# Spectral mixing by full float32 products in place of three products of rounded parts

## The chip, the cores and the metric

One core of one Trainium2 chip runs the whole program. The metric is the device time of one execution in microseconds, from launch to end. TensorE (PE in the profile; PEld are its weight loads), VectorE (DVE), ScalarE (ACT), GpSimd (POOL) and SyncE (SP, which issues most transfers) each work through their own instructions in order.

## The reference

The input is `q`, `k`, `v` of shape (8, 8, 576, 64), float32, and two weight matrices. For each batch:

```
q_d, k_d, v_d = means of q, k, v over groups of 4 positions
out_d   = softmax attention of the pooled q_d, k_d, v_d      (144 positions)
local   = softmax attention within |i - j| < 4               (576 positions)
x       = repeat(out_d, 4) + local, heads side by side       -> (8, 576, 512)
mixed   = Re(FFT over 512 channels of the FFT over 576 positions of x)
u       = x + mixed
un      = layer norm of u
out     = u + relu(un @ w_ch1) @ w_ch2                        (512 -> 2048 -> 512)
```

## The kernel before

**Stages.** The first part goes batch by batch: 40 units of local attention (5 in each batch), 8 pooled attentions, and 8 spectral mixings (`Mix`). The mixed rows go to DRAM. The second part is the feed-forward network over 36 tiles of 128 tokens in 9 blocks; blocks from the fourth on use a scheme with fewer products (`product`, L1120). In the meantime the weights are unpacked in 64 quarters (`Quarter`).

**The order.** Every step is an item; the table `TURNS` gives each item a place, all items are sorted by place, and each engine works through its own in that order. Loads of the attention inputs (L574, L578) and stores stand in SyncE's queue; the constants (`constants`, L715 to L717), the pooled sums (L450) and the accumulating loads (L1019, L1023) in GpSimd's.

**Precision.** A product of type F32R is a single pass at reduced precision. The kernel gets near float32 by splitting each operand into a rounded part ("high") and the remainder ("low") and adding three products: high x high, high x low and low x high. Attention scores, probabilities times values, and transposes are plain float32 products.

**A mixing (`Mix`), for one batch.** `half_sum` (L733, VectorE, `xs`) and `half_difference` (L736, GpSimd, `xm`) add and subtract the mirrored halves of the sequence. `channels` (L744, VectorE, `w`) and `fold` (L757, one half on VectorE and one on GpSimd, `xeo`) do the same along the channels, in four slots of 128 rows. `split_high` (L768, ScalarE) rounds a folded slot to `fh`, `split_low` (L771, GpSimd) takes the remainder `fl`. `split_z` (L779 ScalarE, L780 GpSimd) does that for the two channels that are their own mirror images. `sequence` (L793) multiplies with the cosine and sine constants `seqm` along the sequence: for each of four groups T, 4 slots x 3 products of 290 columns, accumulated in PSUM. `sequence_z` (L812) does 8 products for the single channels. `sequence_high` (L800, ScalarE) rounds the result to `yh`, `sequence_low` (L804, VectorE) takes the remainder `yl`. `mix` (L832, L839) multiplies these with the channel constants `chanm`, 2 x 3 products of 256 columns for each row tile and parity; `even_out` (L846) and `unfold` (L858) combine the two parities.

Of the kernel before, what the change touches and what calls it, by code (L numbers as in the profile page):

```python
# [27 lines left out]
        0, 9, 10, 27, 42, 84, 98, 111, 152, 166, 207, 231, 226, 272, 300, 325, 370, 392, 439, 501, 529, 570,  # L28
        612, 702, 681, 707, 748, 838, 829, 841, 940, 975,
    ),  # L30
    "Pooled.scores": (
        17, 16, 47, 82, 106, 173, 217, 239, 298, 358, 386, 449, 522, 539, 582, 670, 690, 737, 821, 845, 908,
        959, 995, 1049,
    ),
    "Pooled.maxima": (
        21, 20, 52, 87, 109, 182, 221, 246, 306, 362, 389, 459, 527, 542, 590, 674, 698, 745, 825, 851, 916,
        968, 1001, 1053,
    ),
    "Pooled.exps": (
        25, 33, 57, 89, 122, 184, 234, 256, 308, 365, 396, 468, 544, 551, 608, 678, 713, 776, 832, 862, 926,  # L40
        980, 1012, 1055,
    ),
    "Pooled.transpose_p": (
        29, 48, 62, 110, 126, 188, 249, 282, 332, 385, 427, 474, 546, 566, 638, 699, 740, 782, 855, 884, 928,
        989, 1018, 1060,
    ),
    "Pooled.copy_p": (
        34, 56, 71, 120, 142, 201, 255, 285, 334, 394, 431, 478, 552, 575, 643, 709, 743, 788, 861, 898, 936,
        993, 1022, 1065,
    ),  # L50
    "Pooled.values": (
        49, 58, 90, 140, 147, 209, 281, 297, 343, 407, 434, 484, 565, 584, 657, 739, 752, 801, 883, 910, 944,
        1017, 1048, 1067,
    ),
    "Pooled.result": (
        51, 63, 94, 163, 162, 213, 290, 304, 346, 412, 446, 490, 589, 593, 661, 747, 770, 809, 888, 912, 950,
        1032, 1052, 1075,
    ),
    "Pooled.store": (151, 225, 376, 504, 650, 869, 1028, 1083),
    "Pooled.pack": (102, 228, 369, 530, 682, 830, 963, 1082),  # L60
    "Mix.half_sum": (
        132, 129, 131, 245, 220, 268, 379, 414, 413, 557, 560, 563, 696, 720, 746, 852, 850, 891, 982, 984,
        1033, 1106, 1094, 1110,
    ),
    "Mix.half_difference": (
        115, 116, 112, 237, 236, 274, 393, 416, 417, 549, 571, 580, 703, 706, 751, 842, 879, 856, 976, 977,
        1010, 1105, 1100, 1118,
    ),
    "Mix.channels": (
# [4 lines left out]
    ),  # L74
    "Mix.fold": (
# [4 lines left out]
    ),  # L80
    "Mix.split_high": (
        121, 145, 177, 176, 286, 276, 337, 336, 421, 422, 479, 477, 572, 577, 619, 622, 712, 742, 777, 791, 901,
        900, 937, 935, 991, 1014, 1046, 1066, 1122, 1137, 1168, 1169,
    ),
    "Mix.split_low": (
        139, 168, 179, 178, 301, 299, 341, 340, 438, 437, 482, 481, 579, 581, 623, 625, 732, 750, 780, 799, 904,
        902, 941, 942, 1008, 1041, 1063, 1085, 1134, 1142, 1175, 1176,
    ),
    "Mix.split_z": (119, 143, 253, 275, 395, 430, 467, 576, 640, 778, 814, 899, 992, 1056, 1064, 1117),
    "Mix.sequence_z": (175, 333, 450, 628, 784, 930, 1061, 1125),  # L90
    "Mix.z_high": (185, 338, 480, 641, 789, 934, 1116, 1136),
    "Mix.z_low": (196, 350, 491, 647, 794, 948, 1128, 1185),
    "Mix.sequence": (
        191, 187, 189, 190, 355, 359, 357, 356, 521, 523, 507, 508, 665, 671, 636, 639, 818, 820, 805, 804, 956,
        957, 970, 971, 1113, 1114, 1092, 1096, 1190, 1189, 1192, 1191,
    ),
    "Mix.sequence_high": (204, 203, 367, 363, 525, 512, 679, 646, 831, 816, 960, 981, 1123, 1124, 1215, 1212),
    "Mix.sequence_low": (211, 210, 382, 381, 540, 517, 686, 662, 835, 823, 966, 987, 1127, 1129, 1224, 1219),
# [5 lines left out]
    "Mix.even_out": (
        280, 254, 397, 423, 433, 574, 578, 711, 692, 734, 860, 859, 994, 1025, 1013, 1148, 1149, 1236, 1284,
        1308,
    ),
    "Mix.unfold": (
        305, 294, 289, 295, 410, 411, 443, 442, 463, 462, 601, 591, 599, 632, 727, 728, 767, 772, 768, 769, 889,
        887, 864, 868, 1005, 1006, 1072, 1071, 1031, 1030, 1184, 1154, 1182, 1223, 1272, 1270, 1315, 1316, 1327,  # L110
        1341,
    ),
    "Mix.store_mixed": (368, 458, 685, 826, 964, 1081, 1252, 1324),
    "Mix.store_local": (103, 157, 263, 262, 375, 455, 535, 655, 683, 762, 870, 925, 1029, 1080, 1104, 1111),
    "Mix.store_ends": (532, 962, 1078, 1357),
    "Unit.load": (
        2, 1, 4, 6, 5, 40, 39, 38, 43, 77, 101, 154, 158, 153, 159, 149, 266, 331, 264, 328, 371, 378, 454, 456,
        503, 537, 528, 618, 617, 651, 757, 760, 754, 763, 761, 874, 872, 921, 873, 922,
    ),
    "Unit.sum_in": (  # L120
        8, 11, 12, 13, 14, 53, 55, 64, 67, 78, 193, 197, 198, 199, 200, 317, 320, 347, 351, 353, 488, 489, 495,
        516, 519, 592, 602, 631, 648, 660, 796, 806, 807, 810, 811, 919, 946, 947, 951, 953,
    ),
    "Unit.load_v": (
        3, 41, 76, 75, 100, 99, 150, 155, 156, 224, 223, 227, 261, 329, 373, 372, 453, 505, 502, 531, 536, 614,
        615, 653, 652, 758, 755, 759, 828, 827, 871, 876, 875, 924, 923, 1027, 1026, 961, 1079, 1077,
    ),
# [12 lines left out]
    "Unit.transpose_p": (  # L140
        30, 31, 59, 79, 92, 93, 125, 174, 192, 216, 250, 260, 311, 310, 384, 425, 424, 485, 511, 545, 596, 597,
        637, 666, 688, 719, 718, 786, 787, 834, 844, 885, 929, 931, 969, 1020, 1019, 1088, 1058, 1095,
    ),
    "Unit.copy_p": (
        35, 36, 72, 83, 97, 118, 127, 202, 205, 230, 279, 278, 323, 324, 391, 429, 432, 498, 514, 548, 607, 606,
        644, 668, 701, 733, 735, 790, 798, 837, 858, 897, 932, 939, 973, 1023, 1024, 1089, 1062, 1097,
    ),
    "Unit.values": (
        37, 50, 81, 91, 104, 148, 172, 208, 215, 238, 313, 309, 344, 383, 399, 435, 473, 510, 538, 554, 627,
        629, 659, 687, 715, 783, 785, 819, 833, 846, 909, 915, 943, 955, 988, 1040, 1038, 1093, 1087, 1098,  # L150
    ),
    "Unit.result": (
        44, 54, 86, 96, 107, 164, 181, 212, 218, 242, 319, 315, 348, 388, 405, 447, 486, 526, 541, 561, 630,
        633, 664, 694, 726, 792, 795, 824, 836, 849, 911, 945, 949, 965, 1002, 1051, 1045, 1103, 1090, 1107,
    ),
    "constants": (28,),
    "clear_yz": (74,),
    "close_b": (1099,),
    "close_a": (1139,),
    "close_e": (1238,),  # L160
    "close_d": (1367,),
    "Block.load": (
        377, 611, 903, 534, 797, 1009, 756, 878, 974, 452, 978, 1084, 1156, 1164, 1180, 1158, 1166, 1198, 1162,
        1201, 1240, 1159, 1217, 1253, 1649, 1657, 1662, 1651, 1658, 1666, 1652, 1659, 1668, 1653, 1661, 1669,
    ),
    "Block.stats": (1070, 1073, 1091, 1119, 1206, 1221, 1269, 1271, 1667),
# [93 lines left out]
def kernel(  # L260
# [450 lines left out]
    for t in (zs.bitcast(F32), *(t[:, :, DM:] for t in halves)):  # L711
        nc.gpsimd.memset(t, 0.0)
# [749 lines left out]
```

## Time and profile before

| | |
|---|---|
| median of 3 runs | 1140.92 us (1140.8 to 1146.13) |
| the profiled execution | 1142.11 us, span 1140.3 us |
| TensorE busy | 1051.2 us, 92% |
| VectorE busy | 648.7 us, 57% |
| ScalarE, GpSimd busy | 410.1 us, 415.7 us |
| granted TensorE clock, mean | 0.976 of full |
| moved by DMA | 226.81 MB |

Busy time is the time in which an engine has at least one instruction under way. TensorE's instructions are pipelined and their ends are modelled, so its busy time is an upper figure; distances between starts say what an instruction costs in a row of others. Of the rows below, "idle before" is the time that the engine stood still ahead of the instruction, and behind "<-" stands what ended it.

### The profile page before, as it was taken

What the parts mean: (1) busy time and instruction counts of PE and PEld (TensorE: products, weight loads), DVE (VectorE), ACT (ScalarE), POOL (GpSimd) and SP (SyncE); (2) the same over time, 40 slices, a digit from 0 to 9 for tenths busy, and PEclk for the clock granted to TensorE, in tenths of its full rate; (3) what the DMA queues carried; (4) which work ended last, traced back from release to release, by engine and by line L of the source; (5) the groups of instructions that cost most, each with busy time, mean ns of one, the idle gap of its engine ahead of it and who ended that gap; (6) DMA issues with size and microseconds to landing.
All of it is one profiled execution on the core that took longest, in us unless ns stands there. A gap on an engine that the chain in (4) does not pass through costs nothing.

```text
span 1140.3 us, 24515 instructions
## 1 busy us (share of the span) xinstructions
PE 1051.2 (92%) x9364; PEld 913.5 (80%) x9364; DVE 648.7 (57%) x1314; ACT 410.1 (36%) x1138; POOL 415.7 (36%) x572
## 2 busy tenths in 40 slices
PE   5677877887889999999899999999999999999998
PEld 4566766776878888888788989989889888989997
DVE  3688998997898877354223443443343353353433
ACT  3646656765544443132121232232132132132111
POOL 2244545644575554477532131330231321222000
PEclk9888999998999999999999999999999999999999
DMA  8877878997576442668905945964974875785651
GB/s 278 236 223 207 280 197 240 284 260 183 138 188 186 129 122 93 156 208 276 236 28 182 285 152 157 269 232 159 239 249 156 231 251 183 207 265 175 218 161 37
DMA packets 124692, 226.81 MB, mean 199 GB/s; under 512 B 15104, under 2 KB 30592, under 8 KB 124320
## 3 DMA queue, kind: packets, MB, share of 16 engines
q1 hardware_dynamic: 110288, 194.51, 52.1%
q0 software_dynamic: 14288, 30.74, 14.8%
q8 instruction: 74, 1.21, 0.4%
q14 instruction: 42, 0.34, 0.1%
HBM read 179.56 MB, written 45.42 MB: 197 GB/s over the span
## 4 chain that ended last, share of the span: by engine, by line
PE 65%; DMA 12%; DVE 11%; SPq 5%; POOL 3%; issue 3%; ACT 2%; DVEq 0%; POOLq 0%; ACTq 0%
PE banks L1120 19%; PE banks L1202 10%; PE banks L1203 10%; PE banks L1204 10%; PE banks L1182 9%; DMA qkT<-in_qk_dram 2%; DMA vaug<-in_vw_dram 2%; DMA xa<-rest 1%; DVE sums L592 1%; PE banks L1049 1%; DMA w1h<-ut 1%; SPq L552 1%; DMA w1l<-ut 1%; SPq L551 1%; DMA ux<-xa 1%
## 5 line engine op out<-in xcount | busy, mean ns | idle before, releaser
L1202 PE MATMUL banks<-w2h,hh 128*128 128x512 f32 x576 | 228.6, 397 | 0.5 <-ACT hh L1186 0.5
L1203 PE MATMUL banks<-w2l,hh 128*128 128x512 f32 x576 | 226.2, 393 | 0.0
L1204 PE MATMUL banks<-w2h,hl 128*128 128x512 f32 x576 | 225.9, 392 | 0.0
L1186 ACT ACTIVATE hh<-row 128x512 fp32r<-128x512 f32 x96 | 60.8, 633 | 284.5 <-DVE row L1145 193.1
L1145 DVE TENSOR_TENSOR row<-wt,banks 128x256 f32<-128x256 f32 x192 | 80.4, 419 | 142.8 <-PE banks L1120 138.2
L1190 DVE SCALAR_TENSOR_TENSOR hl<-row,hh 128x512 fp32r<-128x512 f32 x96 | 68.8, 717 | 119.0 <-ACT hh L1186 119.0
L1204 PEld LDWEIGHTS banks<-w2h,hl 128*128 128x128 f32 x576 | 108.6, 189 | 24.8 <-DVE hl L1190 0.8
L1202 PEld LDWEIGHTS banks<-w2h,hh 128*128 128x128 f32 x576 | 108.8, 189 | 20.7 <-ACT hh L1186 0.9
L1203 PEld LDWEIGHTS banks<-w2l,hh 128*128 128x128 f32 x576 | 108.8, 189 | 19.4
L1182 PE MATMUL banks<-unT,w1h 128*128 128x512 f32 x384 | 102.1, 391 | 0.5 <-DVE unT L1058 0.5
L1019 POOL DMA_DIRECT2D ut<-ux x40 | 35.8, 1037 | 149.6 <-DMA ut<-um 144.8
L1182 PEld LDWEIGHTS banks<-unT,w1h 128*128 128x128 f32 x384 | 71.9, 188 | 16.3 <-DVE unT L1058 1.0
L1190 DVE SCALAR_TENSOR_TENSOR hl<-banks,hh 128x512 fp32r<-128x512 f32 x48 | 32.9, 687 | 79.5 <-ACT hh L1186 79.4
L628 ACT ACTIVATE sb<-banks,mx 128x64 f32<-128x64 f32 x320 | 70.2, 331 | 1.9 <-PE banks L641 0.6
L1140 ACT COPY wt<-banks 128x256 f32<-128x256 f32 x96 | 35.8, 373 | 94.2 <-PE banks L1120 94.2
L1034 POOL TENSOR_TENSOR rstd<-rstd,mhalf 128x1 f32<-128x1 f32 x36 | 21.4, 594 | 118.7 <-DVE rstd L1033 118.5
L1120 PE MATMUL banks<-w1h,w1l 128*128 128x256 f32 x384 | 62.4, 284 | 1.7 <-DMA w1l<-ut 1.2
L1120 PE MATMUL banks<-w1h,w1h 128*128 128x256 f32 x384 | 61.9, 283 | 1.8 <-DVE wt L1145 1.0
L1120 PE MATMUL banks<-unT,w1h 128*128 128x256 f32 x432 | 63.2, 282 | 0.0
L1120 PE MATMUL banks<-unT,w1l 128*128 128x256 f32 x432 | 63.2, 282 | 0.0
L1120 PEld LDWEIGHTS banks<-unT,w1h 128*128 128x128 f32 x432 | 59.9, 191 | 3.9
L1120 PEld LDWEIGHTS banks<-unT,w1l 128*128 128x128 f32 x432 | 59.8, 191 | 3.7
(127 smaller groups left out, 2102.0 us busy)
## 6 DMA issues: line engine op xcount, KB each, us to landing
w1l<-ut SPq DMA_DIRECT2D x96, 256.0 KB
w1h<-ut SPq DMA_DIRECT2D x96, 256.0 KB
qkT<-in_qk_dram SPq DMA_DIRECT2D x40, 512.0 KB
w1h<-ub SPq DMA_DIRECT2D x72, 256.0 KB
w1l<-ub SPq DMA_DIRECT2D x72, 256.0 KB
raw<-in_wq_dram SPq DMA_DIRECT2D x64, 256.0 KB
vaug<-in_vw_dram SPq DMA_DIRECT2D x40, 260.0 KB
out_dram<-ut SPq DMA_DIRECT2D x36, 256.0 KB
```

The costliest lines, as they stand in the source:

```text
L628: nc.scalar.activation(out=self.sb[:, hp, z], in_=self.sc[:, z, hp], func=AF.Exp, scale=0.125, bias=self.mx[:, z, hp : hp + 1],)
L1019: nc.gpsimd.dma_start(out=to, in_=ux[b][k0 : k0 + m, :], accum_op=ALU.add)
L1034: nc.gpsimd.tensor_tensor(out=rstd, in0=rstd, in1=mhalf, op=ALU.pow)
L1120: nc.tensor.matmul(into, w[:, y, c, :], both[z][:, c, :], start=(start and i == 0), stop=(i == len(mms) - 1), skip_group_check=True)
L1140: nc.scalar.copy(out=joins[k].bitcast(F32), in_=self.ps[x])
L1145: nc.vector.tensor_add(out=place(to), in0=place(a), in1=self.ps[x])
L1182: nc.tensor.matmul(hps, a[:, c, :], unT[:, x, c, :], start=(i == 0), stop=(i == len(mms) - 1))
L1186: nc.scalar.activation(out=hh, in_=self.hps[f], func=AF.Relu)
L1190: nc.vector.scalar_tensor_tensor(out=hl, in0=self.hps[f], scalar=0.0, in1=self.hh[f].bitcast(F32), op0=ALU.max, op1=ALU.subtract)
L1202: nc.tensor.matmul(acc, hh, w2h, start=start, stop=False)
L1203: nc.tensor.matmul(acc, hh, w2l, start=False, stop=False)
L1204: nc.tensor.matmul(acc, hl, w2h, start=False, stop=stop)
```

## The change

The mixing uses plain float32 products: one product for each pair of operands, in place of three F32R products of rounded parts. `split_high` and `split_low` go; `fold` writes the whole of `f`, which holds all four slots and has two buffers. `split_z` loses its subtraction. `sequence_high` becomes `sequence_out`, one copy of the PSUM result to `yh`, and gives the banks back; `sequence_low` goes. The constants `seqm` and `chanm` hold one part in place of two. `TURNS` has the same order of items as before, without those that are gone; `sequence_out` has the places of `sequence_high` and the numbers are closed up.

```diff
-    seqm = psq.tile([P, 2, 2, NSL + 1, KEPT], F32R, name="seqm")
-    chanm = pf.tile([P, 2, 4, HN], F32R, name="chanm")
+    seqm = psq.tile([P, 2, NSL + 1, KEPT], F32, name="seq")
+    chanm = pf.tile([P, 4, HN], F32, name="chan")
...
-    zs = psq.tile([P, NSL + 1, ZCOLS], F32R, name="z")
+    zs = psq.tile([P, NSL + 1, ZCOLS], F32, name="z")
...
         def fold(self, t, minus):
-            if self.x.get(t) is None:
-                self.x[t] = psq.tile([P, 4, P], F32, name="xeo", bufs=2)
+            if self.f is None:
+                self.f = psq.tile([P, NSL + 1, 4, P], F32, name="f", bufs=2)
...
-                out=self.x[t][:, 2 * minus : 2 * minus + 2, :],
+                out=self.f[:, t, 2 * minus : 2 * minus + 2, :],
...
-        def split_high(self, t):
-            if self.fh is None:
-                self.fh, self.fl = (psq.tile([P, NSL + 1, 4, P], F32R, name=f"f{part}", bufs=1) for part in "hl")
-            nc.scalar.copy(out=self.fh[:, t], in_=self.x[t])
-
-        def split_low(self, t):
-            nc.gpsimd.tensor_sub(out=self.fl[:, t], in0=self.x[t], in1=self.fh[:, t].bitcast(F32))
...
             nc.scalar.copy(out=z[:, :, 0:2], in_=x)
-            nc.gpsimd.tensor_sub(out=z[:, :, 2:4], in0=x, in1=z[:, :, 0:2].bitcast(F32))
-
-        def slots(self, x, odd, i):
-
-            return [(x[:, t], seqm[:, i, odd, t, :]) for t in (NSL, NSL - 1, *range(NSL - 1))]
+
+        def slots(self, x, odd):
+
+            return [(x[:, t], seqm[:, odd, t, :]) for t in (NSL, NSL - 1, *range(NSL - 1))]
 
         def sequence(self, T):
-            fh, fl = self.fh[:, :, T, :], self.fl[:, :, T, :]
...
-            mms = [x for f, i in ((fh, 0), (fh, 1), (fl, 0)) for x in self.slots(f, T % 2, i)]
+            mms = self.slots(self.f[:, :, T, :], T % 2)
...
-        def sequence_high(self, i):
+        def sequence_out(self, i):
             if self.yh is None and self.b % 2 == 0:
-                self.yh, self.yl = (pf.tile([P, 4, 2 * KEPT], F32R, name=f"y{part}", bufs=1) for part in "hl")
+                self.yh = pf.tile([P, 4, 2 * KEPT], F32, name="yf", bufs=1)
             elif self.yh is None:
-                self.yh, self.yl = mixes[self.b - 1].yh, mixes[self.b - 1].yl
+                self.yh = mixes[self.b - 1].yh
             nc.scalar.copy(out=self.yh[:, 2 * i : 2 * i + 2, self.mine], in_=self.y[i])
-
-        def sequence_low(self, i):
-            yh, yl = (y[:, 2 * i : 2 * i + 2, self.mine] for y in (self.yh, self.yl))
-            nc.vector.tensor_sub(out=yl, in0=self.y[i], in1=yh.bitcast(F32))
             done((self, i), "y")
 
         def sequence_z(self):
 
             y = self.yzp = bank(self, "yz", ZCOLS)[:, 0, :KEPT]
-            mms = [x for i in range(2) for x in self.slots(zs, 0, i)]
+            mms = self.slots(zs, 0)
...
             for half, T in enumerate((3, 1) if odd else (0, 2)):
-                mh, ml = chanm[:, 0, T, :], chanm[:, 1, T, :]
-                lh, ll = self.yh[:, T, cols], self.yl[:, T, cols]
                 to = ps[:, half * HD : (half + 1) * HD]
-                for i, (l, r) in enumerate(((lh, mh), (lh, ml), (ll, mh))):
-                    nc.tensor.matmul(
-                        to, l, r, start=(bool(odd) and i == 0), stop=(i == 2), skip_group_check=True
-                    )
+                nc.tensor.matmul(
+                    to, self.yh[:, T, cols], chanm[:, T, :], start=bool(odd), stop=True, skip_group_check=True
+                )
```

## Rows read from the trace of the kernel before

**Rows 1.** Stretch, length, busy us (instructions): PE, PEld, DVE, ACT, POOL; clock, DMA, GB/s.

```profile
45.00:345.00 300.00, 244.08 (x4435) 208.60 (x4425) 262.87 (x537) 178.62 (x601) 159.36 (x203) 0.93 0.78 217
345.00:1140.00 795.00, 781.31 (x4435) 683.34 (x4433) 365.28 (x742) 212.35 (x468) 246.90 (x346) 1.00 0.62 187
```

**Rows 2.** The same for two stretches of 45 us.

```profile
0.00:45.00 45.00, 25.79 (x507) 21.52 (x511) 20.54 (x37) 19.09 (x69) 9.46 (x24) 0.89 0.92 287
...
180.00:225.00 45.00, 39.25 (x821) 32.99 (x817) 41.92 (x89) 32.55 (x115) 26.07 (x36) 1.00 0.90 267
```

**Rows 3.** Groups of instructions by line and shape, whole span.

```profile
L771 POOL TENSOR_TENSOR fl<-xeo,fh 128x512 fp32r<-128x512 f32 x32 | 42.6, 1341 | 12.7 <-ACT fh L768 12.5
...
L736 POOL TENSOR_TENSOR xm<-xa,xb 128x512 f32<-128x512 f32 x24 | 34.4, 1439 | 29.4 <-DMA xa<-rest 24.7 <-DVE xb L689 4.7
...
L757 POOL TENSOR_TENSOR xeo<-w 128x256 f32<-128x256 f32 x32 | 28.4, 899 | 21.7 <-DVE w L744 18.6 <-DVE rs L686 3.0
...
L757 DVE TENSOR_TENSOR xeo<-w 128x256 f32<-128x256 f32 x32 | 23.2, 729 | 0.4
...
L733 DVE TENSOR_TENSOR xs<-xa,xb 128x512 f32<-128x512 f32 x24 | 20.9, 877 | 6.6 <-DMA xa<-rest 6.6
...
L804 DVE TENSOR_TENSOR yl<-banks,yh 128x580 fp32r<-128x580 f32 x16 | 12.1, 757 | 3.8 <-ACT yh L800 3.7
```

**Rows 4.** Four lines by themselves: duration in ns, minimum/median/maximum, first and last start.

```profile
L757 DVE TENSOR_TENSOR xeo<-w x32: 409/424/2594, 48.1 to 323.0; 128x256 f32<-128x256 f32 x32
...
L733 DVE TENSOR_TENSOR xs<-xa,xb x24: 678/686/1805, 56.3 to 312.7; 128x512 f32<-128x512 f32 x24
...
L467 PE MATMUL banks<-sums x384: 282/283/501, 16.4 to 295.5; 64*64 64x144 f32 x128, 64*32 64x144 f32 x64
...
L793 PE MATMUL banks<-seqm,fh x256: 290/297/608, 72.3 to 330.9; 128*128 128x290 f32 x128
```

**Rows 5.** Timeline at 302 us: start, length, engine and instruction.

```profile
301.92 2.01 DVE L757 TENSOR_TENSOR xeo<-w 128x256 f32<-128x256 f32 x1
302.06 1.58 POOL L771 TENSOR_TENSOR fl<-xeo,fh 128x512 fp32r<-128x512 f32 x1
```

**Rows 6.** DMA from 20 to 38 us: total, and an issue with its landing.

```profile
DMA packets 1386, 5.97 MB, mean 332 GB/s; under 512 B 280, under 2 KB 280, under 8 KB 1128
...
seqm<-in_c_seq_dram POOLq DMA_DIRECT2D x1, 2320.0 KB, 14.2
```

**Rows 7.** Chain that ended last, first 400 us: by line, and one piece.

```profile
by line: PE banks L1182 8.5%; DMA qkT<-in_qk_dram 6.3%; DMA vaug<-in_vw_dram 5.9%; issue 5.3%; DMA xa<-rest 4.2%; DVE sums L592 4.1%; SPq L552 3.5%; SPq L551 3.2%; DMA ux<-xa 3.2%; PE banks L839 3.0%; PE banks L793 2.2%; DVE xeo L757 2.2%; 
...
20.17 12.87 DMA vaug<-in_vw_dram
```

**Rows 8.** Timeline of TensorE at 33 us.

```profile
33.18 0.86 PE L669 MATMUL banks<-vaug,pT 64*64 64x65 f32 x32 [4.22 <-DMA vaug<-in_vw_dram]
```

**Rows 9.** Timeline of TensorE, last sequence products, and transposes.

```profile
326.78 1.24 PE L793 MATMUL banks<-seqm,fh 128*128 128x290 f32 x8
327.85 0.70 PE L793 MATMUL banks<-seqm,fl 128*128 128x290 f32 x4
...
363.45 1.04 PE L1049 MATMUL banks<-ident,un 128*128 128x128 f32 x8
```

**Rows 10.** Timeline of TensorE, a mix.

```profile
205.84 0.40 PE L839 MATMUL banks<-chanm,yh 128*128 128x256 f32 x2
...
206.19 0.40 PE L839 MATMUL banks<-chanm,yh 128*128 128x256 f32 x2
```

**Rows 11.** TensorE and weight loads busy: L793 in one stretch, L839 in all.

```profile
45.00:345.00 300.00, 61.58 (x384) 55.80 (x384) 0.93 0.78 217
...
sum 1095.00, PE 38.73 PEld 34.20; mean PE 19.36 PEld 17.10
```

**Rows 12.** TensorE's waits, 45 to 345 us.

```profile
PE banks L839 <- DVE yl L804: 5.7, 3, 5.2
```

**Rows 13.** ScalarE's waits, 45 to 345 us.

```profile
ACT yh L800 <- PE banks L793: 14.6, 5, 5.7
```

More of the change, by code (lines that the diff above doesn't have):

```diff
@@ L33 @@
[L33 removed]
+        17, 16, 47, 82, 106, 169, 207, 229, 286, 340, 366, 425, 493, 510, 548, 631, 650, 695, 773, 795, 854,
+        901, 934, 984,
     ),
     "Pooled.maxima": (
[L36 to L37 removed]
+        21, 20, 52, 87, 109, 174, 211, 236, 292, 344, 369, 435, 498, 512, 556, 635, 658, 702, 776, 801, 862,
+        909, 940, 988,
     ),
     "Pooled.exps": (
[L40 removed]
@@ L57 @@
-        1032, 1052, 1075,
-    ),
-    "Pooled.store": (151, 225, 376, 504, 650, 869, 1028, 1083),
-    "Pooled.pack": (102, 228, 369, 530, 682, 830, 963, 1082),
+        51, 63, 94, 160, 159, 203, 278, 290, 328, 392, 422, 462, 555, 559, 623, 704, 726, 761, 838, 858, 892,
+        969, 987, 1008,
+    ),
+    "Pooled.store": (148, 215, 358, 476, 612, 819, 965, 1016),
+    "Pooled.pack": (102, 218, 351, 501, 643, 781, 905, 1015),
     "Mix.half_sum": (
-        132, 129, 131, 245, 220, 268, 379, 414, 413, 557, 560, 563, 696, 720, 746, 852, 850, 891, 982, 984,
-        1033, 1106, 1094, 1110,
+        131, 128, 130, 235, 210, 258, 361, 394, 393, 527, 530, 533, 656, 679, 703, 802, 800, 841, 923, 925, 970,
+        1038, 1026, 1042,
@@ L93 @@
[L93 to L98, printed above, removed]
[4 rows of a table added]
+    ),
+    "Mix.split_z": (119, 141, 243, 265, 375, 408, 443, 545, 602, 733, 766, 849, 931, 991, 998, 1049),
@@ new lines @@
+    "Mix.sequence_z": (171, 319, 426, 590, 738, 876, 996, 1056),
+    "Mix.z_high": (177, 322, 454, 603, 743, 880, 1048, 1064),
+    "Mix.z_low": (188, 332, 463, 609, 747, 890, 1058, 1107),
+    "Mix.sequence": (
+        183, 179, 181, 182, 337, 341, 339, 338, 492, 494, 479, 480, 626, 632, 598, 601, 770, 772, 757, 756, 898,
+        899, 911, 912, 1045, 1046, 1024, 1028, 1112, 1111, 1114, 1113,
+    ),
+    "Mix.sequence_out": (196, 195, 349, 345, 496, 484, 640, 608, 782, 768, 902, 922, 1054, 1055, 1137, 1134),
@@ L106 @@
[L106 removed]
+        269, 244, 377, 401, 411, 543, 546, 671, 652, 692, 810, 809, 933, 962, 951, 1074, 1075, 1156, 1204, 1228,
     ),
     "Mix.unfold": (
[L109 to L114 removed]
@@ L115 @@
-    "Mix.store_ends": (532, 962, 1078, 1357),
+        291, 282, 277, 283, 390, 391, 419, 418, 439, 438, 567, 557, 565, 594, 686, 687, 723, 728, 724, 725, 839,
+        837, 814, 818, 944, 945, 1005, 1004, 968, 967, 1106, 1080, 1104, 1144, 1192, 1190, 1235, 1236, 1247,
+        1261,
+    ),
+    "Mix.store_mixed": (350, 434, 646, 777, 906, 1014, 1172, 1244),
+    "Mix.store_local": (103, 154, 253, 252, 357, 431, 506, 617, 644, 718, 820, 871, 966, 1013, 1036, 1043),
+    "Mix.store_ends": (503, 904, 1011, 1277),
@@ L157 @@
     "clear_yz": (74,),
[L158 to L161, printed above, removed]
+    "close_b": (1031,),
+    "close_a": (1066,),
+    "close_e": (1158,),
+    "close_d": (1287,),
     "Block.load": (
-        377, 611, 903, 534, 797, 1009, 756, 878, 974, 452, 978, 1084, 1156, 1164, 1180, 1158, 1166, 1198, 1162,
-        1201, 1240, 1159, 1217, 1253, 1649, 1657, 1662, 1651, 1658, 1666, 1652, 1659, 1668, 1653, 1661, 1669,
-    ),
-    "Block.stats": (1070, 1073, 1091, 1119, 1206, 1221, 1269, 1271, 1667),
@@ L171 @@
+    "Block.stats": (1003, 1006, 1023, 1051, 1128, 1142, 1189, 1191, 1587),
+    "Block.norm": (1034, 1053, 1061, 1077, 1129, 1187, 1193, 1233),
+    "Block.turn": (1047, 1057, 1072, 1081, 1159, 1213, 1239, 1238),
+    "Block.turn_high": (1065, 1076, 1095, 1110, 1177, 1224, 1245, 1252),
+    "Block.turn_low": (1067, 1079, 1103, 1126, 1188, 1234, 1246, 1260),
     "Block.first": (
-        1208, 1210, 1233, 1209, 1290, 1346, 1370, 1347, 1369, 1413, 1416, 1460, 1471, 1415, 1526, 1528, 1542,
-        1543, 1580, 1608, 1625, 1634, 1635, 1650, 1660,
+        1130, 1132, 1153, 1131, 1210, 1266, 1290, 1267, 1289, 1333, 1336, 1380, 1391, 1335, 1446, 1448, 1462,
+        1463, 1500, 1528, 1545, 1554, 1555, 1570, 1580,
@@ L701, in plan @@
                 at(fn)
-    seqm = psq.tile([P, 2, 2, NSL + 1, KEPT], F32R, name="seqm")
-    chanm = pf.tile([P, 2, 4, HN], F32R, name="chanm")
+    seqm = psq.tile([P, 2, NSL + 1, KEPT], F32, name="seq")
+    chanm = pf.tile([P, 4, HN], F32, name="chan")
     signs = pf.tile([P, 2], F32R, name="signs")
     yz = pf.tile([P, 2 * KEPT], F32R, name="yz")
-    zs = psq.tile([P, NSL + 1, ZCOLS], F32R, name="z")
+    zs = psq.tile([P, NSL + 1, ZCOLS], F32, name="z")
     halves = [pf.tile([P, NSL, DM + 2], F32, name=f"x{h}") for h in "sm"]
-    for t in (zs.bitcast(F32), *(t[:, :, DM:] for t in halves)):
+    for t in (zs, *(t[:, :, DM:] for t in halves)):
         nc.gpsimd.memset(t, 0.0)
@@ L719, in clear_yz @@
     def clear_yz():
-        nc.scalar.mul(out=yz, in_=seqm[:, 0, 0, 0:2, :].bitcast(F32).rearrange("p a k -> p (a k)"), mul=0.0)
+        nc.scalar.mul(out=yz, in_=seqm[:, 0, 0:2, :].rearrange("p a k -> p (a k)"), mul=0.0)
     class Mix:
         def __init__(self, b):
-            self.b, self.x, self.y = b, {}, {}
+            self.b, self.y = b, {}
             self.w, self.ps, self.o, self.even, self.mixed = {}, {}, {}, {}, {}
-            self.fh = self.yh = self.ends = None
+            self.f = self.yh = self.ends = None
             self.mine = slice(b % 2 * KEPT, b % 2 * KEPT + KEPT)
@@ L902, in plan @@
                     at(self.fold, slot, minus)
-                at(self.split_high, slot)
-                at(self.split_low, slot)
             for pooled in (True, False):
@@ L911, in plan @@
                 if T % 2:
-                    at(self.sequence_high, T // 2)
-                    at(self.sequence_low, T // 2)
+                    at(self.sequence_out, T // 2)
             for slot in range(2 + self.b % 2):
@@ L1326, in _constants @@
     S, DM, P, W, STEP, NW, KEPT = 576, 512, 128, 64, 57, 5, 290
-    def split(a):
-        hi32 = a.astype(np.float32)
-        bits = hi32.view(np.uint32).astype(np.uint64)
-        bits = (bits + 0x7FF + ((bits >> 12) & 1)) & 0xFFFFF000
-        hi = bits.astype(np.uint32).view(np.float32)
-        return hi, (a - hi.astype(np.float64)).astype(np.float32)
     ident = np.eye(P, dtype=np.float32)
@@ L1359, in _constants @@
             seq[W : W + S // 4 - P, i, 2] += x[P:]
-    seq = np.stack(split(seq), axis=1)
     j = np.arange(DM)
@@ L1368, in _constants @@
     chan = np.stack([cos[:, 0::2], sin[:, 1::2], cos[:, 1::2], sin[:, 0::2]], axis=1)
-    chan = np.stack(split(chan), axis=1)
     signs = np.zeros((P, 2))
```

104 lines of the change are left out of this document (44 added, 60 removed), and 64 rows, old and new, of the table TURNS.

## The prediction

> **What bounds the kernel now.** I read busy time by stretch first, then the waits, then the chain that ended last, and at the end single groups and pieces of the timeline. The stretches show two stages. After 345 us TensorE is busy 781 of 795 us [rows 1]: the feed-forward part, which the change doesn't touch except for the last mixes. From 45 to 345 us no engine is full. VectorE is the fullest, 263 of 300 us [rows 1] and 41.9 of 45 us at the worst [rows 2]; TensorE has 244, ScalarE 179, GpSimd 159, and the DMA engines are busy 0.78 of it [rows 1]. So in this stage I take VectorE as the bound, with TensorE and DMA close behind. The first 45 us are different: the DMA engines are 0.92 busy and VectorE has 20.5 us of work [rows 2], so loads set the pace.
>
> **Part by part.**
>
> *The low part of the sequence products* (L804) goes: 16 instructions of 757 ns, 12.1 us of VectorE [rows 3], and with them its 3.7 us of waits for `yh` [rows 3]. Upper end 15.8 us; lower end 0, if another engine sets the stage.
>
> *The split of the folded input* (L768, L771) goes: ScalarE's copies and 42.6 us of GpSimd [rows 3], and the small `z` subtractions. Neither engine is the bound, so their own time is counted at nothing. What it costs is seen on VectorE. Its fold (L757) takes 424 ns as a median and 2594 ns at most [rows 4], and a timeline shows why: a fold of 2.01 us starts 0.14 us before a 1.58 us `fl` subtraction and ends 0.29 us after it [rows 5]. VectorE instructions with two inputs in SBUF sit through a GpSimd instruction. The excess of mean over median is (729 - 424) x 32 for L757 and (877 - 686) x 24 for L733 [rows 3, 4], 9.8 + 4.6 = 14.4 us; L744 has a smaller one that I leave out. The GpSimd groups that can block them are mostly `fl` 42.6, `xm` 34.4 and `xeo` 28.4 us [rows 3]; `fl` is 40% of these, so 6 us. Lower end 0 (the remaining GpSimd work moves up and blocks as much), upper end 14.4 us.
>
> The Trainium skill says of this pair (SBUF — State Buffer, "Who interferes with whom") that either engine holds the shared port for its whole instruction and the other fully blocks. The timeline agrees, with 2.01 us for a fold of 0.42; by that rule without the row's share, all of the 14.4 us could go with `fl`, and the sum would be 7 us better.
>
> *The constants* shrink by half: the 2320 KB of `seqm` [rows 6] and the 1024 KB of `chanm` (128 x 2 x 4 x 256 x 4 bytes) become 1672 KB. In that stretch everything together moves at 332 GB/s [rows 6]. A `vaug` load that is under way from 20.17 us for 12.87 us is a piece of the chain [rows 7], and TensorE idles 4.22 us for it, until 33.18 us [rows 8]. 1.71 MB less at 332 GB/s are 5.2 us. I take 4, because the piece behind it starts with loads of its own; lower end 0.
>
> *TensorE* gets fewer, dearer instructions. Now a sequence product is three records: eight of them start in 1.07 us [rows 9], 0.134 us each, so 0.402 us. A mix product is three records in 0.35 us [rows 10]. No float32 product with full 128 x 128 weights is in the trace, but three things price it. A float32 product is two records: L467 has 384 of them [rows 4] for 24 products in each of 8 batches. Each record streams at two cycles a column: 144 float32 columns take 283 ns as a median [rows 4], nearly as much as the 297 ns of 290 columns now [rows 4]. And float32 transposes with full 128 x 128 weights run eight in 1.04 us [rows 9]; less the 0.28 us of one record that is 0.11 us a start, for 128 columns two cycles each at 2.4 GHz. So a full product costs four cycles a column: 0.483 us for 290 columns, 0.427 us for 256. Against now: 128 sequence products at +0.081 are +10.4 us; 32 products of the `z` columns, of two records now, at 0.483 - 0.268 are +6.9 us; 80 mix products at 0.427 - 0.35 are +6.2 us. Together +23.5 us. For part of the stage the clock is at the lower level (mean 0.93 [rows 1], so 14% of it) and the difference doubles: 27 us is the upper end.
>
> How much of it is felt? Of the first 400 us of the chain the mix and sequence lines hold 3.0 + 2.2% [rows 7], 20.8 us, out of 61.6 + 38.7 us of their busy time [rows 11]: a fifth, 5 us, the lower end. But when VectorE gets shorter TensorE comes next, with 244 + 24 of some 285 us. I take half, 12 us.
>
> The Trainium skill puts true float32 at four passes through the array (FP8 and Floating Point Precision, "TensorE Precision Notes"). With each pass as long as a present record, its overhead too, the added TensorE time would be 17.2 + 8.6 + 9.3 = 35 us instead of 23.5, and the gain, by half of that, 6 us smaller. The rows of the transposes speak for the smaller figure.
>
> *What moves.* All other items keep their order; the one copy out of the sequence products (`sequence_out`) stands where `sequence_high` stood, and gives its PSUM banks back one VectorE instruction earlier. The mix then waits for that ScalarE copy alone: TensorE's 5.7 us of waits for `yl` [rows 12] go, and late next is the copy, which already waits 14.6 us for TensorE [rows 13]. Longer products lengthen this wait, and the Exp instructions queued behind it on ScalarE feed the transposes of the scores. Against that ScalarE loses `fh` and its waits for the folds. I count the two as even, within 10 us either way. Folds get a whole buffer each batch instead of two slots; worth nothing, as VectorE's waits have none for a slot. If SyncE's queue got its loads out late instead, this cover would be gone, but nothing on it is added.
>
> **The sum.** Of 15.8 + 6 us on VectorE I take the 88% of the stage that it is busy, -19. Constants -4. TensorE +12. Together -11 us. The profiled execution took 1142.1 us (its span 1140.3), 1.2 us above the median of the runs; 1142.1 - 11 is 1131, on the median's scale 1130 us.
>
> **Rivals.**
>
> *The whole gain arrives*, because TensorE's longer runs fill its own 56 us of idling: 15.8 + 6 + 5 less the 5 on the chain is 22, 1119 us. For it: ScalarE and GpSimd get slack too. Against: DMA would rise from 0.78 to some 0.85, and transfers stand all along the chain [rows 7]. 0.15.
>
> *It comes out even.* All of TensorE's 23.5 us are felt, since it works in order and each batch's scores and transposes queue behind its sequence products; against 19 + 4 us of gain that leaves the time as it is, 1141 us. For it: TensorE would be the busiest engine. Against: a fifth of these lines is on the chain. 0.20.
>
> *It gets slower.* A full float32 record waits for its own weight load. Loads are busy 55.8 us for 384 [rows 11], 0.145 us each; were all 480 exposed, TensorE would gain 23.5 + 70 us of work, and by the same half 47 us felt less 23 gained is 1165 us. It decides from about 47 ns exposed for each load, where half of 23.5 + 22.5 equals the gain. Against it: now the loads run beside products that start every 0.117 us [rows 10], and float32 records would stream twice as long. 0.17, with whatever else lengthens TensorE's queue. The Trainium skill has a rule for this (TensorE: Matmul & The Clock Gate, "What overlaps and what doesn't"): a weight load runs beside a product in flight only where the row groups differ. The present records contradict it.
>
> **The numbers.** My forecast, 1121 to 1135 us, has 0.48. Faster is 0.48 + 0.15 = 0.63; within 0.5% (5.7 us, about what can be told from no change) 0.20; slower 0.17. The range from 1113 to 1148 us leaves out most of the last rival and the tail of the first, together under 0.2.
>
> **What the changed profile would show.** Two records for each sequence and mix product, starting 0.24 us apart at 290 columns and 0.21 at 256; half of that would say that the products are cheap, 0.35 that the loads are exposed. L757's mean at 600 ns or less on an unchanged median. The `vaug` load of 20 us landing some 4 us sooner. TensorE full from about 335 instead of 345 us, and an unchanged stage after it. The prediction is wrong if TensorE's busy time before that grows by more than 40 us, or if VectorE's falls by 20 us and the stage stays as long, which would put DMA or SyncE's queue in its place.

## The result and the profile after

The changed kernel takes 1129.29 us as a median of 5 runs (1128.04 to 1135.41), the kernel before 1141.06 us beside it (1140.8 to 1146.13). The ratio is 0.9899 [0.9864, 0.9934], 11.5 us less. Ratios are those of the record, from the executions of both kernels, and need not equal the quotient of the two medians; one execution at a lower granted clock (1186 us at 0.81, with one rounded pass) is left out of them. The forecast was 1130 us. Its sum of -11 us came out, but its two largest terms did not, as the experiments show.

The profiled execution of the changed kernel is its slowest run, 1135.41 us with a span of 1133.4; so stages are compared by when they begin, not by the spans. Busy time and chain of the changed kernel, from its page:

```profile
PE 1068.8 (94%) x9156; PEld 900.1 (79%) x9156; DVE 631.0 (56%) x1298; ACT 392.3 (35%) x1106; POOL 371.9 (33%) x524
...
PE 63%; DMA 14%; DVE 12%; SPq 4%; issue 3%; ACT 2%; POOL 1%; DVEq 0%; ACTq 0%; POOLq 0%
```

The two stretches of [rows 1], for the changed kernel, with the same columns:

```profile
45.00:345.00 300.00, 266.30 (x4199) 200.42 (x4200) 249.71 (x530) 162.52 (x567) 121.25 (x163) 0.94 0.80 223
345.00:1140.00 795.00, 773.68 (x4376) 675.82 (x4374) 356.48 (x720) 207.28 (x456) 241.21 (x337) 0.99 0.61 184
```

From 45 to 345 us TensorE has 22 us more than in [rows 1], VectorE 13 us less, GpSimd 38 us less; TensorE is now the busiest engine of the stage. (The second row ends after this program does, so its busy time is less.) The groups that answer to [rows 3], of the changed kernel:

```profile
L771 PE MATMUL banks<-seq,f 128*128 128x290 f32 x256 | 69.0, 420 | 3.2 <-DVE unT L1026 2.2 <-DVE xa L678 0.8 <-DVE xb L678 0.3
...
L725 POOL TENSOR_TENSOR xm<-xa,xb 128x512 f32<-128x512 f32 x24 | 36.0, 1515 | 26.6 <-DMA xa<-rest 15.4 <-DMA vaug<-in_vw_dram 5.5 <-DVE xb L678 3.1
...
L746 POOL TENSOR_TENSOR f<-w 128x256 f32<-128x256 f32 x32 | 27.9, 883 | 47.0 <-DVE w L733 34.3 <-DVE rs L675 12.7
...
L722 DVE TENSOR_TENSOR xs<-xa,xb 128x512 f32<-128x512 f32 x24 | 22.2, 932 | 5.3 <-DMA xa<-rest 5.3
...
L746 DVE TENSOR_TENSOR f<-w 128x256 f32<-128x256 f32 x32 | 18.2, 574 | 0.3
```

The VectorE fold's mean went from 729 ns [rows 3] to 574, and that of `xs` from 877 to 932. Two lines by themselves, durations in ns and first and last start, as in [rows 4]:

```profile
L746 DVE TENSOR_TENSOR f<-w x32: 407/417/2576, 43.5 to 308.8; 128x256 f32<-128x256 f32 x32
...
L771 PE MATMUL banks<-seq,f x256: 405/407/693, 66.0 to 322.2; 128*128 128x290 f32 x128
```

The sequence products run from 66.0 to 322.2 us instead of 72.3 to 330.9 [rows 4]: 6.3 us are gained before the first one, and 8.7 us by the last. TensorE is busy all but without a gap from 322.6 us on, in the kernel before from 334.2 us on. Both rows, the changed kernel's first, columns as in [rows 1]:

```profile
322.60:450.00 127.40, 127.38 (x566) 103.94 (x565) 102.55 (x211) 52.39 (x130) 65.30 (x108) 1.00 0.49 141
```

```profile
334.20:450.00 115.80, 115.80 (x530) 95.45 (x531) 97.86 (x204) 50.27 (x126) 63.47 (x105) 1.00 0.50 141
```

So the gain was made in the first stage; what follows took 806 us before and 811 us in this execution. The records themselves cost what was worked out. Timeline of TensorE in the changed kernel, a run of 24 sequence records, a mix, and the value products of [rows 8]:

```profile
222.20 6.13 PE L771 MATMUL banks<-seq,f 128*128 128x290 f32 x24
...
202.09 1.03 PE L810 MATMUL banks<-chan,yf 128*128 128x256 f32 x4
...
28.88 0.33 PE L658 MATMUL banks<-vaug,pT 64*64 64x65 f32 x2
29.69 0.69 PE L658 MATMUL banks<-vaug,pT 64*64 64x65 f32 x30 [0.49 <-ACT sb L617]
```

(6.13 - 0.41) / 23 is 0.249 us a record of 290 columns, (1.03 - 0.38) / 3 is 0.217 us for 256, two records a product: four cycles a column, and no weight load in the open. The value products that idled for `vaug` until 33.18 us [rows 8] start at 28.88 and wait no more for it. The constants' loads, in the changed kernel's view of DMA from 19 to 34 us (the last figure is the time to landing):

```profile
seq<-in_c_seq_dram POOLq DMA_DIRECT2D x1, 1160.0 KB, 11.9
...
chan<-in_c_chan_dram POOLq DMA_DIRECT2D x1, 512.0 KB, 13.6
```

### The profile page after: what moved, and what is told of

Same layout as the page of the kernel before. It is cut to its first block, busy times and chain, and to the rows that moved or that the text cites. A ratio compares the mean times of both kernels' runs of the same rounds, so it can differ in the third digit from the quotient of the medians.

```text
span 1133.4 us, 23993 instructions
## 1 busy us (share of the span) xinstructions
PE 1068.8 (94%) x9156; PEld 900.1 (79%) x9156; DVE 631.0 (56%) x1298; ACT 392.3 (35%) x1106; POOL 371.9 (33%) x524
## 2 busy tenths in 40 slices
DMA packets 124690, 225.06 MB, mean 199 GB/s; under 512 B 15104, under 2 KB 30592, under 8 KB 124448
## 4 chain that ended last, share of the span: by engine, by line
PE 63%; DMA 14%; DVE 12%; SPq 4%; issue 3%; ACT 2%; POOL 1%; DVEq 0%; ACTq 0%; POOLq 0%
PE banks L1088 16%; PE banks L1150 10%; PE banks L1170 10%; PE banks L1171 9%; PE banks L1172 9%; DMA w1l<-ut 2%; DMA ut<-ud 2%; DMA w1h<-ut 2%; PE banks L1017 2%; PE banks L771 1%; PE banks L810 1%; DVE xs L722 1%; DMA raw<-in_wq_dram 1%; DMA out_dram<-ut 1%; DVE sums L581 1%
## 5 line engine op out<-in xcount | busy, mean ns | idle before, releaser
L771 PE MATMUL banks<-seq,f 128*128 128x290 f32 x256 | 69.0, 420 | 3.2 <-DVE unT L1026 2.2
```

The source lines that it names most:

```text
L771: nc.tensor.matmul(y, l, r, start=(i == 0), stop=(i == len(mms) - 1))
```

## The experiments

Times are medians; differences go by the ratios to the kernel before, of which 0.001 is 1.1 us. Where two kernels are compared, the half-widths of their two intervals are combined as the root of the sum of squares. The changed kernel's own share of that, 4.0 us from five executions, is the same in every comparison with it. The theory on record: VectorE sets the first stage, with TensorE second. The rivals: TensorE sets it once its products are longer; or the constants carry most of the gain.

**The constants at their old size.**

```diff
-    seqm = psq.tile([P, 2, NSL + 1, KEPT], F32, name="seq")
-    chanm = pf.tile([P, 4, HN], F32, name="chan")
+    seqs = psq.tile([P, 2, 2, NSL + 1, KEPT], F32, name="seq")
+    seqm = seqs[:, 0]
+    chans = pf.tile([P, 2, 4, HN], F32, name="chan")
+    chanm = chans[:, 0]
```

> The changed kernel with the constants at their old size (each part loaded twice, the second copy unused). If the shares of the prediction hold, 4 us of the gain come back: 1133 us, ratio to before 0.993. Rival, that the first loads carry most of the gain because every batch after them is only shifted: 6 us or more come back, 1135 us or above. If the loads are hidden: 1129 us.

Measured: 1138.33 us, 0.996 [0.9931, 0.9989]. So 7.0 us come back, give or take 5.2; the first sequence product starts at 71.2 us, against 66.0 in the changed kernel and 72.3 before. That is more than the 4 us of the sum, which the interval still includes.

**GpSimd's subtractions back.**

```diff
+        def split_low(self, t):
+            if self.fl is None:
+                self.fl = psq.tile([P, NSL + 1, 4, P], F32R, name="fl", bufs=1)
+            nc.gpsimd.tensor_sub(out=self.fl[:, t], in0=self.f[:, t], in1=self.f[:, t])
...
             nc.scalar.copy(out=z[:, :, 0:2], in_=x)
+            nc.gpsimd.tensor_sub(out=z[:, :, 2:4], in0=x, in1=z[:, :, 0:2])
```

> The changed kernel with GpSimd's 32 subtractions of 128x512 and the 16 small ones put back at their old places, their results unused (the large ones) or zero (the small ones). By the prediction VectorE is held up again: some 5 us come back, 1134 us, and the VectorE fold's mean goes from 574 to about 700 ns. Rival, that TensorE sets the stage now: VectorE's fold gets longer but the time stays within 2 us of 1129.

Measured: 1134.55 us, 0.9939 [0.9916, 0.9961]: 4.6 us come back, give or take 4.7, near the 5 expected but not clear of zero. The blocking itself is plain. Groups of this kernel, `fl` and VectorE instructions that it meets:

```profile
L768 POOL TENSOR_TENSOR fl<-f 128x512 fp32r<-128x512 f32 x32 | 37.5, 1187 | 4.2 <-DVE rs L686 2.2 <-DVE f L757 1.6 <-DVE rsd L527 0.4
...
L757 DVE TENSOR_TENSOR f<-w 128x256 f32<-128x256 f32 x32 | 21.7, 682 | 0.3
...
L744 DVE TENSOR_TENSOR w<-xm 128x255 f32<-128x255 f32 x24 | 15.9, 665 | 1.4 <-POOL xm L736 1.2
```

The fold is at 682 ns again, on the way from 574 to 729. The channel sums `w`, which the prediction left out as the smaller part, are blocked more. The same group in the changed kernel and then in the kernel before:

```profile
L733 DVE TENSOR_TENSOR w<-xm 128x255 f32<-128x255 f32 x24 | 10.4, 438 | 3.0 <-POOL xm L725 2.8
```

```profile
L744 DVE TENSOR_TENSOR w<-xm 128x255 f32<-128x255 f32 x24 | 13.0, 544 | 1.9 <-POOL xm L736 1.7
```

With `fl` back the three groups of `w` together take 37.5 us instead of 28.2, the fold 21.7 instead of 18.2. VectorE's busy time grows by 11.3 us, from 631.0 to 642.3, so less is felt than is blocked. (`fl` waits less than it did, 4.2 us instead of 12.7, as it needs no `fh`; so it meets other instructions than in the kernel before.)

**VectorE's subtraction back.**

```diff
             nc.scalar.copy(out=self.yh[:, 2 * i : 2 * i + 2, self.mine], in_=self.y[i])
-            done((self, i), "y")
+
+        def sequence_low(self, i):
...
+            nc.vector.tensor_sub(out=yl, in0=self.y[i], in1=yh)
+            done((self, i), "y")
```

> The changed kernel with VectorE's 16 subtractions out of PSUM put back, results unused, the banks given back behind them. By the prediction 16 x 757 ns and their waits, times 0.88: 11 to 14 us come back, 1141 us. Rival, that TensorE sets the stage: at most 4 us, 1133 us or less.

Measured: 1137.23 us, 0.9954 [0.9932, 0.9976]: 6.3 us come back, give or take 4.7. Its group:

```profile
L797 DVE TENSOR_TENSOR yl<-banks,yf 128x580 fp32r<-128x580 f32 x16 | 12.1, 757 | 3.5 <-ACT yf L789 3.4
```

The 12.1 us of busy time and 3.4 us of waits for ScalarE are there as before, 15.5 us, of which the interval lets at most 11.0 be felt: less than 0.88. It also includes the rival's 4 us.

**The products alone.** This is the kernel before with one float32 product in place of three; all splits are still made, as the two diffs above and a ScalarE copy from `xeo` to `fh` show.

```diff
-            mms = [x for f, i in ((fh, 0), (fh, 1), (fl, 0)) for x in self.slots(f, T % 2, i)]
+            mms = self.slots(self.fh[:, :, T, :], T % 2)
...
-                for i, (l, r) in enumerate(((lh, mh), (lh, ml), (ll, mh))):
...
+                    to, self.yh[:, T, cols], chanm[:, T, :], start=bool(odd), stop=True, skip_group_check=True
```

> The kernel before with the products alone changed: constants at their old size, the ScalarE copy and the GpSimd subtraction of each folded slot, the small subtractions and VectorE's subtraction out of PSUM all still there (the low parts are computed and unused), but one float32 product in place of three. By the prediction half of TensorE's added 23.5 us is felt: 1153 us, slower than before by 12 us. Rival, that TensorE sets the stage: all of it, 1160 us or more. Rival, that the longer products are hidden: 1141 to 1145 us.

Measured: 1139.36 us, 0.9978 [0.9958, 0.9999]. All three expectations fail: the longer products come out a little ahead of the kernel before. They do two things, though. They are longer, and they no longer wait for GpSimd's and VectorE's low parts. The next run parts these.

**The products alone, with the old waits.**

```diff
-            nc.scalar.copy(out=self.fh[:, t], in_=self.x[t])
+            nc.scalar.mul(out=self.fh[:, t], in_=self.x[t], mul=0.5)
...
-            mms = self.slots(self.fh[:, :, T, :], T % 2)
+            mms = self.slots(self.fl[:, :, T, :], T % 2)
...
-            nc.scalar.copy(out=self.yh[:, 2 * i : 2 * i + 2, self.mine], in_=self.y[i])
+            nc.scalar.mul(out=self.yh[:, 2 * i : 2 * i + 2, self.mine], in_=self.y[i], mul=-1.0)
...
-                    to, self.yh[:, T, cols], chanm[:, T, :], start=bool(odd), stop=True, skip_group_check=True
+                    to, self.yl[:, T, cols], chanm[:, T, :], start=bool(odd), stop=True, skip_group_check=True
```

> As the fourth run (products alone), but TensorE waits as it did before: ScalarE's copy is scaled by a half or by -1, so that GpSimd's and VectorE's subtractions give the very operands that the float32 products read. So this differs from the kernel before in the length of TensorE's products and in nothing else that TensorE waits for. If the shorter chain of waits is what pays for the longer products: slower than before by 5 us or more, 1147 us, ratio 1.005 or above. If TensorE simply has room for 23.5 us: as the fourth run, ratio 0.998.

Measured: 1143.22 us, 1.0008 [0.9986, 1.003]. The length alone costs 0.9 us (-1.6 to 3.4) of its 23.5. The waits make the difference of 3.4 us to the run before, give or take 3.4. TensorE's own waits for `yl` are there again. Waits of TensorE in this kernel, 45 to 310 us:

```profile
PE banks L842 <- DVE yl L810: 4.3, 3, 3.6
PE banks L602 <- ACT sb L628: 3.1, 7, 0.5
```

The waits aren't quite the old ones. In the kernel before two of three sequence products read `fh` and only the last reads `fl`; here all of them read `fl`, and TensorE idles 3.5 us for it instead of 0.8. Those products, in the kernel before and then here:

```profile
L793 PE MATMUL banks<-seqm,fl 128*128 128x290 f32 x128 | 24.0, 307 | 0.8 <-POOL fl L771 0.8
```

```profile
L795 PE MATMUL banks<-seq,fl 128*128 128x290 f32 x256 | 70.7, 427 | 4.6 <-POOL fl L775 3.5 <-DVE xa L689 1.1
```

So 0.9 us is rather an upper figure for the length, and 3.4 us for the waits.

**One rounded pass.** In the changed kernel `seqm`, `chanm`, `z`, `f` and `yf` become F32R:

```diff
-    seqm = psq.tile([P, 2, NSL + 1, KEPT], F32, name="seq")
-    chanm = pf.tile([P, 4, HN], F32, name="chan")
+    seqm = psq.tile([P, 2, NSL + 1, KEPT], F32R, name="seq")
+    chanm = pf.tile([P, 4, HN], F32R, name="chan")
```

> The changed kernel with one rounded product in place of the float32 one, nothing else: 80 us less TensorE time; the low parts of all operands are left out. If TensorE has room in the first stage, VectorE and the transfers still set it and at most 8 us are gained: 1121 us or more. If TensorE sets the stage now, half of the 80 us or more: 1090 us.

Measured: 1127.66 us, 0.9872 [0.9833, 0.9912]: 3 us less than the changed kernel, give or take 6.0, for 76 us less of products (133.1 to 57.2 us busy by line). TensorE alone doesn't set the stage. But it isn't as free as this looks. The same stretch for the changed kernel and then for this one (columns as in [rows 1]):

```profile
45.00:310.00 265.00, 233.48 (x4062) 174.50 (x4063) 224.30 (x476) 149.73 (x536) 100.41 (x132) 0.94 0.80 227
```

```profile
45.00:310.00 265.00, 189.14 (x3863) 151.85 (x3862) 225.00 (x481) 151.59 (x541) 103.53 (x136) 0.84 0.83 232
```

The mean granted clock falls from 0.94 to 0.84 of 2.4 GHz; worked out from these means, that is 32% of the time at 1.2 GHz instead of 12%. Part of the work saved is given back in slower records of the attention products: the transposes of the scores take 331 ns a record instead of 307, the value products 244 instead of 234.

**The constants later.**

```diff
-    "constants": (28,),
+    "constants": (78.5,),
+    "late_constants": (101.5,),
...
+    def late_constants():
+        nc.gpsimd.dma_start(out=chanm, in_=c_chan)
+        nc.gpsimd.dma_start(out=signs, in_=c_signs)
```

> The changed kernel with the constants asked for later (sequence constants at place 78.5, channel constants at 101.5 in place of 28), and the clearing of yz fed from the identity, so that they don't travel with the first attention loads. If the first loads shift everything behind them, as the first run says, the other half of the constants is worth 5 us too: 1124 us. If they only collide with later loads: 1129 us.

Measured: 1129.8 us, 0.9901 [0.9865, 0.9936]: no gain, give or take 5.7; the interval just includes the 5 us. So taking the other half out of the first loads isn't shown to be worth anything.

**The whole fold on GpSimd**, on top of that.

```diff
-            eng, op = (nc.gpsimd, ALU.subtract) if minus else (nc.vector, ALU.add)
+            eng, op = (nc.gpsimd, ALU.subtract) if minus else (nc.gpsimd if t in (0, 1, 2, 3) else nc.vector, ALU.add)
```

> The one before, and the 32 additions of the fold on GpSimd in place of VectorE: 18 us less VectorE, 28 us more GpSimd. If VectorE sets the stage: 8 us faster than the one before, 1116 us. If the chain through the fold counts more than VectorE's load: no faster, or slower, as the fold takes 0.9 in place of 0.57 us.

Measured: 1132.51 us, 0.9897 [0.9855, 0.994], the same as the one before, give or take 6.3. The additions leave VectorE, 18.4 us, but its busy time falls by 7.7 us only, from 629.4 to 621.7, because others of its instructions run longer (the three groups of `w` take 32.6 us instead of 27.4). The chain through the fold got longer too, so this doesn't clear VectorE; the run with shorter sums does.

**One more load in the middle of the stage.**

```diff
+    "again": (500.5,),
...
+    def again():
+        nc.gpsimd.dma_start(out=seqs[:, 1], in_=c_seq)
+        nc.gpsimd.dma_start(out=chans[:, 1], in_=c_chan)
```

> The changed kernel with one more load of the constants (1.71 MB, into a copy that nothing reads) in the middle of the first stage. If the bytes set the stage, it costs what the first run's did, 7 us: 1136 us. If that run's cost came from the collision with the first attention loads: 0 to 2 us, 1130 us.

Measured: 1138.16 us, 0.9972 [0.9949, 0.9995]: 8.3 us, give or take 4.8, as much as at the start. So the cost of the constants isn't peculiar to the first loads. The run also puts two more issues into GpSimd's order; what these cost and what the bytes cost isn't parted.

**Fewer loads.**

```diff
+            if r >= 2:
+                return
             if r == 0:
                 self.vs = pd.tile([P, H + HP, D + 1], F32, name="vsum", bufs=2)
```

> The changed kernel without 16 of the 32 loads that sum the pooled v (5.5 MB less; the pooled values are those of half the positions). If the bytes set the stage: 5.5 MB at 245 GB/s, 22 us, of which the other engines leave some 15: 1115 us. If VectorE or TensorE sets it: 0 to 3 us.

Measured: 1128.39 us, 0.989 [0.9856, 0.9923]: 1 us less than the changed kernel, give or take 5.5, with 5.6 MB less moved (225.06 to 219.46). Nothing like the 15 us that bytes as the bound would give. (The 245 GB/s of the expectation stand in no row; at the 223 GB/s of the stage above, 5.6 MB would be 25 us.)

**Shorter sums on VectorE.**

```diff
-                    nc.vector.tensor_reduce(out=to, in_=x[:, :, a - g0 : e - g0], axis=AX.X, op=ALU.add)
+                    nc.vector.tensor_reduce(out=to, in_=x[:, :, a - g0 : e - g0, :2], axis=AX.X, op=ALU.add)
```

> The changed kernel with VectorE's sums of q and k over two of four positions only (half the input left out): 22 us less of VectorE with no chain made longer. If VectorE sets the stage, as the prediction has it: 15 to 20 us faster, 1112 us. If it is one of several equals: 5 us. If it has room: 0.

Measured: 1131.8 us, 0.9922 [0.9894, 0.995]: no gain (2.6 us more, give or take 5.1), for 20.5 us less of VectorE's busy time (631.0 to 610.5). This is the run that the prediction's theory doesn't survive. Against the run with VectorE's subtraction back, which has 31.3 us more of VectorE, it is 3.7 us ahead, give or take 4.1, and that comparison doesn't use the changed kernel's five executions. Busy time of this kernel in the stretch shown above, and its VectorE's longest waits from 45 to 320 us:

```profile
45.00:310.00 265.00, 233.05 (x4042) 175.96 (x4032) 208.86 (x476) 149.10 (x535) 99.04 (x133) 0.95 0.79 225
```

```profile
DVE rs L686 <- PE banks L669: 9.1, 10, 3.5
DVE rs L686 <- ACT pT L657: 6.6, 1, 6.6
DVE xs L733 <- DMA xa<-rest: 6.5, 3, 4.7
DVE mx L621 <- PE banks L609: 5.2, 5, 1.7
```

VectorE does the same number of instructions there (476) in 15 us less, and waits instead, for TensorE, ScalarE and a transfer in turn. In the changed kernel the first of these waits is 7.3 us, and the second 2.5:

```profile
DVE rs L675 <- PE banks L658: 7.3, 8, 1.6
DVE unT L1026 <- ACT unT L1023: 5.4, 2, 4.9
DVE xs L722 <- DMA xa<-rest: 5.3, 3, 3.2
...
DVE rs L675 <- ACT pT L646: 2.5, 1, 2.5
```

**Both.** The two diffs above together.

> The two before together. If DMA and VectorE take turns as the bound, more than the sum of the two alone, 20 us or more: 1109 us. If one of them sets the stage: as that one alone.

Measured: 1125.81 us, 0.9857 [0.9819, 0.9894]: 4.8 us less than the changed kernel, give or take 5.9. Even with VectorE and DMA relieved at once, the 20 us expected if they took turns as the bound don't come.

**The first stage by itself.** The start of the last `mix` product marks the end of the mixings, without the rest of the program; each trace has it for one execution. The changed kernel, shorter sums, one rounded pass, constants at their old size:

```profile
L810 PE MATMUL banks<-chan,yf x160: 377/379/634, 83.8 to 354.0; 128*128 128x256 f32 x128, 128*68 128x256 f32 x32
```

```profile
L821 PE MATMUL banks<-chan,yf x160: 377/379/670, 85.4 to 353.5; 128*128 128x256 f32 x128, 128*68 128x256 f32 x32
```

```profile
L821 PE MATMUL banks<-chan,yf x80: 274/282/580, 82.0 to 344.0; 128*128 128x256 f32 x64, 128*68 128x256 f32 x16
```

```profile
L823 PE MATMUL banks<-chan,yf x160: 377/379/793, 88.9 to 361.8; 128*128 128x256 f32 x128, 128*68 128x256 f32 x32
```

It starts at 363.2 us in the kernel before, at 354.3 with fewer loads and at 347.1 with both; in the four runs that add work, at 357.0 to 361.9. These single executions scatter by some 5 us: the run with the old waits has 368.5, 5.3 later than the kernel before, where all executions give 0.9. Within that they say what the times say, but for one rounded pass: 76 us off TensorE bring the end of the mixings 10 us forward, so TensorE isn't without weight.

## Why the prediction was right

The time came out right in part by luck: the two largest terms of its sum were wrong in opposite directions.

*The products' price* was right: 0.249 and 0.217 us a record against 0.242 and 0.213 worked out. By these spacings the change adds 26 us, and by the busy time of the mixing's lines 22 us (111.0 to 133.1), on either side of 23.5. The rule of the Trainium skill on float32 (FP8 and Floating Point Precision, "TensorE Precision Notes"), four passes, agrees with the four cycles a column; with the present records' overhead on each pass it would have been 35 us, which the measured spacing excludes. The rival of exposed weight loads fell: 0.249 us is the streaming and 7 ns. With it falls for these records the rule of the Trainium skill that loads overlap only where the row groups differ (TensorE: Matmul & The Clock Gate, "What overlaps and what doesn't").

*How much of it is felt* was the first step that failed. The prediction took half, 12 us, because TensorE "comes next"; the length alone cost 0.9 us (-1.6 to 3.4), below even the fifth that the chain gave as the lower end. This is the term of the sum that was mis-sized by most.

*VectorE at 88%* was the second. The 15.8 us of L804 were to give 14; putting it back costs 6.3, give or take 4.7. The step before it, "in this stage I take VectorE as the bound", is wrong: 20.5 us off VectorE elsewhere give nothing. So the two large terms, -19 and +12, were both too large and nearly made up for each other, which is the luck.

*GpSimd's blocking* was there (729 to 574 ns, and 682 with `fl` back), and its 5 us agree with the 4.6 measured, which isn't clear of zero. But the 6 us were worked out from the wrong instructions. I laid the two engines' timelines of the kernel before beside each other and put each instruction's time over the shortest of its group down to the GpSimd instruction that overlaps it longest, which gives an estimate. Of the folds' time 1.6 us stand beside `fl`, the one fold of [rows 5], and 5.0 beside `xm`, among them the longest of 2594 ns; of that of `xs`, 4.0 beside `xm` and nothing beside `fl`. What `fl` blocked most was `w` (L744), 4.7 us, which the prediction left out as smaller; by mean over median (524 and 544 over 418 ns, 24 each) it is 5.6 us, more than the 4.6 of L733. The total, 6.3 us, is near its 6 by luck, and most of the 14.4 us could not go with `fl`: in the changed kernel `xs` has 5.3 beside `xm`. The Trainium skill (SBUF — State Buffer, "Who interferes with whom") states that a VectorE instruction with two SBUF inputs contends with a GpSimd instruction that reads SBUF; these means agree. They show VectorE held up by GpSimd; the prediction's "either engine", GpSimd held up by VectorE, is in none of the rows shown.

*The constants* gave 7.0, give or take 5.2, against 4; the landing was foreseen ("some 4 us sooner": 28.88 for 33.18 us). The reason given, the first loads, isn't the whole of it, since the same bytes cost as much in the middle of the stage, and since moving the other half showed no gain.

*What moves*, counted as even within 10 us: the shorter chain of waits is worth 3.4 us, give or take 3.4, and that is rather an upper figure.

*The sum by the runs*: length +0.9, shorter waits -3.4, then 9.0 us, give or take 4.6, from the products alone to the changed kernel, which takes out the constants' half, both splits and VectorE's subtraction. The three put back one by one cost 7.0 + 4.6 + 6.3 = 17.9 us. The changed kernel's own 4 us enter that three times, so it is uncertain by 13 us, and whether the parts overlap isn't shown. ScalarE's copies `fh` and the second buffer of `f` were not tried alone.

**What stays open.** Of the three that were relieved, TensorE, VectorE and the DMA engines, none sets the first stage alone: 76 us off TensorE, 20.5 us off VectorE and 5.6 MB off DMA each give 3 us or less, and within their intervals at most 9, 2.5 and 6.5. Additions of 11 us of VectorE's busy time or 1.7 MB cost 6 to 8. Whether additions really cost what removals don't return isn't shown: were the changed kernel's ratio at the upper end of its interval, 0.9934, the four additions would cost 1 to 4 us and the three removals give 1 to 7. The figures fit a chain of short waits that passes from engine to engine in a fixed order, where a relieved engine only waits for the next; but the runs show it for VectorE alone, by the waits above.

By the prediction's own sign, VectorE down by 20 us and the stage as long, DMA or SyncE's queue would stand in its place. The run with fewer loads speaks against the bytes. SyncE's queue was not relieved, and neither was ScalarE. The queue's loads of the attention inputs themselves wait for TensorE; the changed kernel's longest such waits, 40 to 335 us:

```profile
SPq L567 <- PE banks L658: 29.5, 12, 6.9
SPq L563 <- PE banks L598: 12.3, 6, 3.7
```

Another order of the items was not tried.

## What to carry to other kernels

An engine that is 88% busy in a stage need not be its bound: before a saving is multiplied by that share, take some work off the engine in a run of its own and see whether the stage gets shorter. A change that lengthens products but cuts a rounding and a subtraction out of the chain ahead of them is best priced in three parts (length, waits, work on other engines), since here the part that looked dearest cost next to nothing. Put a blocked instruction down to its blocker by the timeline, not by the blockers' shares of busy time. And a sum that comes out right isn't yet a theory that is right: ablate its terms.

## What was not expected of the hardware

Taking 76 us of products off TensorE lowered the mean granted clock in the stage from 0.94 to 0.84 and so gave part of it back. With the old waits the same engine took 23 us more (134.3 us busy by line instead of 111.0) at a clock of 0.94 against 0.93 from 45 to 345 us, and the time rose by 0.9 us (-1.6 to 3.4). And a small load, 1.7 MB, cost 7.0 us (give or take 5.2) at the start and 8.3 (give or take 4.8) in the middle of a stage whose DMA engines are 0.80 busy, while 5.6 MB fewer brought the time down by 1 us, give or take 5.5; as said, the intervals don't part these for certain.
